# Order of loads on one DMA queue: the G load first in its group, weight rows a stage later, the first tile of the last pass in parts

## The chip, the cores and the metric

One core of a Trainium2 chip runs the whole program in one launch. The metric is device time in microseconds (us). PE is the matmul engine (PEld its weight loads), DVE the vector engine, ACT the scalar engine, POOL and SP the two others. SP does no arithmetic here: it issues DMAs, in the order of its instruction list. A DMA issued by SP or ACT goes through that engine's hardware queue, one issued by POOL through the software queue.

## The reference

The function returns the output of a forward pass and the gradients of all its inputs.

```python
def _fwd_reference(A_u, ..., B_w1, B_w3, B_w2):
    x = A_u                                   # [1, 2048, 576] bf16
    xn = _layernorm(x, axis=-1)
    s = _A_ref(xn, A_re, A_im, B_re, B_im, C_re, C_im, log_dt, Dskip)   # long convolution, 128 states
    g = _silu(_B_ref(xn, B_w1, B_w3, B_w2))   # FFN: (silu(xn w1) * (xn w3)) w2, F = 4608
    return x + s * g

def reference(...):
    _out, _vjp = jax.vjp(_f, ...)
    _grads = _vjp(grad_out)
    return (_out, *_grads)
```

The part that matters here is the backward pass of the FFN. With the stored G = xn w1 and U = xn w3 and the gradient `go` of the FFN's output it forms gh = go w2^T, from it the gradients GG and GU of G and U (with silu and its derivative), the weight gradients xn^T GG, xn^T GU and h^T go, and at last, token tile by token tile, GG w1^T + GU w3^T, which is added to the gradient from the convolution and sent through the layernorm's backward. Beside it run the sums for the gradients of the convolution's parameters.

## The kernel before, in words

2048 tokens are 16 tiles of 128; F = 4608 is 36 blocks of 128. The forward pass, in which G and U are written to DRAM (`G_dram`, `U_dram`), and the convolution's backward come first. The change lies in `backward` (L1519) and `phase6_inputs` (L1875), the last 650 us or so.

**The groups.** F is cut into NG = 18 groups of 256 columns (two blocks). In group `gi`, `phase6_group` (L1756) is a generator that yields named stages:

- h0 to h3: `make(s)` multiplies the output gradient `goT` with the group's transposed w2 (`w2T`, L1778, PE), ACT copies the result (L1781), DVE multiplies it into `gu` and `gg` (L1796);
- stored: two stores each of GU and GG to `GU_dram` and `GG_dram` (L1801);
- out_11_c and out_10_c, with marks out_11 and out_10: the weight gradients with the xn tiles (L1850, PE), each copied by ACT (L1852) and stored (`out_dram<-gw`);
- end: the last 64 rows of both (L1859, L1861), copied by ACT (L1864) and stored by `tail` (`out_dram<-gw13t`).

Between the stages the loop in `backward` puts in: the w2 gradient (`phase6_grad2`, L1819, copy by ACT L1823), the loads for later groups, the preparation of the next group (`phase6_prep`: ACT's Silu L1746 and its derivative L1749 on the next group's G, DVE's products L1742, L1743), and the steps of the parameter sums. The Silu of the next group is issued at h3, on ACT ahead of the copies of the stages that follow. PE writes these through two accumulators, which those copies empty.

**Buffers.** `gg_n`, `h_n` and `gu_n` each have two homes, taken in turn by the groups. In the last pass the same homes hold pieces of the transposed weights.

**Parameter sums.** 36 channels, each with two halves. `param_step` (L1230) issues a half: eight matmuls (L1398) with qT and gz, and DVE's product and sum (L1403, L1406) with pz. `param_loads` (L1377) loads qT (a DMA transpose), gz (two loads) and pz for a channel; after a channel's second half the channel two further on is loaded. From group 10 on (GP = 11) there are two to five halves in a group, and more in the last pass. At the end of the last group two such loads are held back, and `param_flush` issues them in the last pass.

**The order on SP.** From group GP - 1 = 10 on, `self.chain` makes every DMA that goes through `sp` follow the one before it in program order, and `one_queue` sends G, U and the gradient stores through SP too. A gradient store is put in a list and issued at the next stage (`stores_due`). The G load of the next group, which `phase6_load` (L1722) asks for at the start of a group, is also put off, to stage h0, where it comes behind the stores that are due:

```python
if stage == "h0" and self.gg_due:
    self.gg_due()
    self.gg_due = None
```

**wA and the pieces.** For the last pass w1 and w3 are needed transposed (block f as 128 x 576). Blocks 0 to 14 of w1 and 0 to 10 of w3 (`wA`) are loaded by rows of 128 (`load_wT_rows`), one chunk at stage end of each of groups 11 to 15. The other blocks come in pieces (`load_piece`) of 7 or 2 blocks, into homes as they come free in the last two groups and behind them. `load_acts` loads GG and GU of a token tile, transposed, as one DMA each of 36 blocks.

**The last pass.** `phase6_inputs` takes the tiles in the order 1, 3, 5, ..., 0, 2, ... For each, `product` runs 72 blocks x 2 column halves (L1899) into two accumulators. The first tile goes through the pieces in the order in which they stand in the list `wT`, up to `ready` = 49 blocks, then 14 more, then, after the first half of the second tile, the rest; later tiles take w1 then w3. `stops` are the blocks behind which a parameter half is put in. The output side (L1938 to L1971) and the blocks of the parameters' end (`phase5_step`, with `X_b`, `ST`, `WO_b`, whose DMAs go through POOL) run beside it.

## Time and profile before

| | us |
|---|---|
| runs | 1776.41, 1776.74, 1767.19 |
| median | 1776.41 |
| profiled execution | 1769.44 |
| its span | 1767.7 |
| PE busy, DVE busy, ACT busy, POOL busy | 1638.1, 1358.4, 937.4, 314.4 |
| granted clock of TensorE, mean | 0.988 |

The span is what the profile covers; the 1.7 us between it and the profiled execution's time lie around it. In rows of a timeline the first two numbers are start and length in us; a bracket at the end gives the idle time of that engine ahead of the row and what ended it. SPq rows are the issue of a DMA by SP, its waits included, not the transfer. In the profile L1899 is the product of the last pass, L1850 the weight gradients, L1693 every DMA transpose, L1717 the G load, L1828 the gradient stores, L1801 the stores of GG and GU.

### The profile page before, as it was taken

Reading aid. Unit: us, or ns where it says so; the run is one execution under the profiler, and the core shown is the slowest. Engines: PE = TensorE matmul, PEld = TensorE weight load, DVE = VectorE, ACT = ScalarE, POOL = GpSimd, SP = SyncE. Lnnn points to the kernel's source line nnn. Section 1 sums busy time; section 2 is a strip of 40 time slices with the busy share of each in tenths; the row PEclk is TensorE's granted clock in tenths of the full one; section 3 lists DMA queues with packets and bytes.
Section 4 is the critical chain, followed back from the end, with each engine's and each line's share of the span. In section 5 each row is a group of like instructions: output and inputs, shape, how many; then the busy total and the mean of one; then the engine's idle time right before and its main releaser. Section 6 shows DMA issues by size and latency. Waiting matters only on the chain. (4 is left out here: it accounts for less than half of the span.)

```text
span 1767.7 us, 35351 instructions
## 1 busy us (share of the span) xinstructions
PE 1638.1 (93%) x13849; PEld 1207.7 (68%) x13909; DVE 1358.4 (77%) x2102; ACT 937.4 (53%) x1757; POOL 314.4 (18%) x516
## 2 busy tenths in 40 slices
PE   7789988999999999999989899999898988999998
PEld 3445544544535777788878788878787876787886
DVE  8778888796783554988966989569797974888775
ACT  5789999976863112776746676555444511010101
POOL 3112222223134110111111101000000033031132
PEclk9999999999999999999999999999999999999999
DMA  7789998889699998867664756589897999999994
GB/s 221 269 268 366 349 355 302 307 267 298 224 274 244 228 204 188 218 206 214 193 189 153 221 167 207 168 225 244 204 239 198 225 244 236 224 219 240 219 213 93
DMA packets 644286, 411.98 MB, mean 233 GB/s; under 512 B 424422, under 2 KB 590934, under 8 KB 639510
## 3 DMA queue, kind: packets, MB, share of 16 engines
q1 hardware_dynamic: 593740, 303.40, 67.2%
q0 software_dynamic: 27632, 87.21, 15.3%
q10 hardware_dynamic: 22746, 19.10, 4.1%
q8 instruction: 109, 1.79, 0.4%
q14 instruction: 59, 0.48, 0.1%
HBM read 130.88 MB, written 190.89 MB: 182 GB/s over the span
## 5 line engine op out<-in xcount | busy, mean ns | idle before, releaser
L1899 PEld LDWEIGHTS <-acts 128*128 128x128 bf16 x2304 | 225.8, 99 | 69.5 <-issue 7.6
L1850 PEld LDWEIGHTS <-xn_bf 128*128 128x128 bf16 x2304 | 225.9, 98 | 56.9 <-issue 29.4
L1403 DVE TENSOR_TENSOR pr_q<-et_ps,pz 128x1024 f32<-128x1024 f32 x144 | 176.0, 1222 | 58.6 <-PE et_ps L1398 45.9
L1899 PE MATMUL px<-wT,acts 128*128 128x288 bf16 x1472 | 192.9, 289 | 7.4 <-DMA wT<-in_B_w_dram 7.4
L1032 PEld LDWEIGHTS <-xnT 128*128 128x128 bf16 x1152 | 107.0, 98 | 112.5 <-issue 24.5
L1406 DVE TENSOR_REDUCE S_all<-pr_q 128x32 f32<-128x1024 f32 x144 | 175.3, 1217 | 3.3
L1778 PE MATMUL ph<-w2T,goT 128*128 128x256 bf16 x1440 | 171.7, 273 | 3.1 <-ACT gh L1781 3.1
L1850 PE MATMUL pgw<-gu_n,xn_bf 128*128 128x256 bf16 x1152 | 137.0, 276 | 23.2 <-ACT gw L1823 19.7
L1032 PE MATMUL pg<-wmB_w,xnT 128*128 128x512 bf16 x545 | 149.1, 379 | 7.7 <-ACT g_t L1048 4.8
L1778 PEld LDWEIGHTS <-goT 128*128 128x128 bf16 x1440 | 139.7, 98 | 20.5 <-issue 4.3
L1819 PE MATMUL pgw<-go_o,h_n 128*128 128x288 bf16 x1152 | 152.3, 287 | 0.2 <-DVE h_n L1743 0.2
L1032 PE MATMUL pu<-wmB_w,xnT 128*128 128x512 bf16 x553 | 149.8, 379 | 0.8
L1819 PEld LDWEIGHTS <-h_n 128*128 128x128 bf16 x1152 | 112.6, 98 | 28.7 <-issue 0.8
L1850 PE MATMUL pgw<-gg_n,xn_bf 128*128 128x256 bf16 x1152 | 130.2, 273 | 1.2 <-ACT gw L1852 1.2
L1781 ACT CAST gh<-ph 128x512 bf16<-128x512 f32 x144 | 82.4, 603 | 77.9 <-PE ph L1778 66.2
L1955 ACT ACTIVATE go<-gx 128x576 bf16<-128x576 f32 x16 | 10.9, 683 | 209.0 <-DVE gx L1938 180.5
L1046 ACT ACTIVATE s_t<-pg 128x512 bf16<-128x512 f32 x144 | 87.9, 611 | 58.3 <-PE pu L1040 36.3
L1899 PE MATMUL px<-wA,acts 128*128 128x288 bf16 x832 | 109.1, 287 | 4.0 <-DMA acts<-GU_dram 2.7
L679 ACT ACTIVATE cs_k<-et_ps 128x512 bf16<-128x512 int16 x216 | 111.5, 637 | 0.1
L1742 DVE TENSOR_TENSOR gg_n<-gg_n,h_n 128x1024 bf16<-128x1024 bf16 x72 | 48.5, 684 | 57.0 <-ACT gg_n L1749 57.0
L1830 POOL DMA_DIRECT2D out_dram<-gw x40 | 26.2, 655 | 349.9 <-ACT gw L1852 166.3
L1060 POOL DMA_DIRECT2D U_dram<-u_t x72 | 51.8, 720 | 203.9 <-ACT u_t L1051 197.0
(315 smaller groups left out, 3231.2 us busy)
## 6 DMA issues: line engine op xcount, KB each, us to landing
U_dram<-u_t POOLq DMA_DIRECT2D x72, 256.0 KB, 4.9
H_dram<-h_t SPq DMA_DIRECT2D x72, 256.0 KB, 5.2
G_dram<-g_t POOLq DMA_DIRECT2D x72, 256.0 KB, 5.0
Q_dram<-q_k SPq DMA_DIRECT2D x36, 512.0 KB, 5.0
GG_dram<-gg_n SPq DMA_DIRECT2D x36, 512.0 KB, 9.9
GU_dram<-gu_n SPq DMA_DIRECT2D x36, 512.0 KB, 5.0
E_dram<-E_k SPq DMA_DIRECT2D x54, 256.0 KB, 2.5
E_l<-E_dram SPq DMA_DIRECT2D x36, 384.0 KB, 6.5
```

Of the source, the lines that this page charges most:

```text
L679: self.sin_last = nc.scalar.activation(out=CS[:, :, o:o + 256], in_=pt[:].bitcast(I16)[:, :, 0::2], func=ACT.Sin, scale=6.283184 / 2 ** 16)
L1032: ins = nc.tensor.matmul(pt[:], lhsT=xnT[:, c, ts], rhs=wm[w][:, c, :], start=(q == 0 and c == 0), stop=(q == 1 and c == nfull - 1))
L1046: nc.scalar.activation(out=s_t[:, :, q, :], in_=pgv, func=ACT.Silu)
L1060: self.u_stores[step] = nc.gpsimd.dma_start(out=dst[fb * ng:(fb + 1) * ng, :, i0:i0 + NT, :].rearrange("g p t f -> p g (t f)"), in_=src[:] ...
L1403: nc.vector.tensor_tensor(out=pr[:].rearrange("p r k e -> p r (k e)"), in0=T[x][:].rearrange("p z k h j a -> p (z k h j a)")[:, None].to_b ...
L1406: nc.vector.tensor_reduce(out=self.S_all[:].rearrange("p r (h c) -> p r h c", h=2)[:, :, :, d0:d0 + 2], in_=pr[:].rearrange("p r k (h j a) ...
L1742: nc.vector.tensor_tensor(out=gg[:, sl, :], in0=gg[:, sl, :], in1=hn[:, sl, :], op=ALU.mult)
L1778: self.pe_last = nc.tensor.matmul(ph[j][:, k, :].rearrange("p (a f) -> p a f", f=P), lhsT=lw, rhs=rh, start=(n == 0), stop=(n == nfull))
L1781: self.sc(lambda: nc.scalar.copy(out=gh[:, j], in_=ph[j][:]))
L1819: self.pe_last = nc.tensor.matmul(pgw[pi_][:, 0:pw], lhsT=hn[:, tt, fl * P:(fl + 1) * P], rhs=go_o[:, tt, po:po + pw], start=(tt == 0), st ...
L1850: self.pe_last = nc.tensor.matmul(pw_[:, 0:FG], lhsT=self.xn_bf[:, tt, c * P:(c + 1) * P], rhs=nat[:, tt, :], start=(tt == 0), stop=(tt == ...
L1899: self.pe_last = nc.tensor.matmul(px[pi_][:, 0:pw], lhsT=acts[i][:, ai, fi, :], rhs=w[:, po:po + pw], start=(n == 0), stop=(n == len(steps ...
```

## The change

1. The G load of the next group is issued at once when `phase6_load` asks for it, at the start of a group. On SP it then stands ahead of the stores that are due there.
2. The chunks of `wA` go from stage end of group g to stage h1 of group g + 1. On SP they stand behind the G load and the `gw13t` stores.
3. The first parameter channel is loaded at stage h2 of group 10, not behind the stores; the second stays.
4. `one_queue` ends with group 16: the gradient stores of the last group go through POOL.
5. GG and GU of the first tile of the last pass: blocks 0 to 33 of GG at h3 of the last group, those of GU behind the stores of the group, then the two last blocks of each.
6. The list of pieces is sorted up to its last four, w1 first, so that the first tile takes all early blocks of w1 before w3. GU of the second tile is loaded ahead of the last two pieces of w3 (blocks 11, 12 and 29 to 35).
7. `param_flush(1)` comes behind GU of the third tile, and the stops of the third tile are 20, 36, 52, 66.

The instructions of the engines stay as they are, but for two more DMA transposes, and on PE and DVE the first parameter half stands earlier.

```diff
-        FA = 12
...
-        FA, GP = 14, 11
+        GP, FE = 11, FT - self.FG // P
...
             for gi in range(NG):
-                self.chain = self.one_queue = gi >= GP - 1
                 lastg = gi == NG - 1
+                self.chain, self.one_queue = gi >= GP - 1, GP - 1 <= gi < NG - 1
...
                     self.stores_due()
-                    if stage == "h0" and self.gg_due:
-                        self.gg_due()
-                        self.gg_due = None
...
-                    if stage == "end" and 0 <= gi - GP < cfg.DT:
+                    if stage == "h1" and 0 <= gi - GP - 1 < cfg.DT:
                         for part in wT[0:2]:
-                            self.load_wT_rows(part, gi - GP)
+                            self.load_wT_rows(part, gi - GP - 1)
...
+                    if stage in ("h2", "stored") and gi == GP - 1:
+                        ch = int(stage == "stored")
+                        self.loaded[ch] = self.param_loads(ch)
                     if stage == "stored":
-                        if gi == GP - 1:
-                            for ch in range(2):
-                                self.loaded[ch] = self.param_loads(ch)
                         if lastg:
                             self.hold = []
                             self.phase5_turn()
-                            acts = [self.load_acts(0)]
+                            self.load_acts(0, (1,), acts[0], 0, FE)
+                            self.load_acts(0, (0, 1), acts[0], FE)
...
                         step()
+                        if lastg and stage == "h3":
+                            acts = [self.load_acts(0, (0,), None, 0, FE)]
...
             self.load_piece(wT, inp, "gg_n", 0, 29, 7)
+            self.load_acts(1, (1,), acts[1])
             self.load_piece(wT, wp, "w2T", 1, 11, 2)
             self.load_piece(wT, inp, "gu_n", 1, 29, 7)
-            self.load_acts(1, (1,), acts[1])
-            self.one_queue = False
-            self.stores_due()
+            wT[:-4] = sorted(wT[:-4], key=lambda part: part[0])
...
-    def load_acts(self, i, parts=(0, 1), t=None):
+    def load_acts(self, i, parts=(0, 1), t=None, f0=0, f1=None):
...
         for k in parts:
-            self.nat_transpose(t[:, k], (self.GG_dram, self.GU_dram)[k][self.order[i]])
+            self.nat_transpose(t[:, k, f0:f1], (self.GG_dram, self.GU_dram)[k][self.order[i]][:, f0 * P:(f1 or self.cfg.FT) * P])
...
         if self.one_queue:
-            self.gg_due = lambda: self.sp(lambda: self.nc.sync.dma_start(out=gg[:], in_=self.G_dram[gi]))
+            self.sp(lambda: self.nc.sync.dma_start(out=gg[:], in_=self.G_dram[gi]))
...
             acts.append(self.load_acts(2, (0,), acts[0]))
-            self.param_flush(1)
             product(1, opened[1][0], 0, cfg.FT, ())
             product(0, opened[0][0], n2, n3, ())
             self.load_acts(2, (1,), acts[0])
+            self.param_flush(1)
             acts.append(self.load_acts(3, (0,), acts[1]))
...
-                stops = ... (12, 28, 44, 62) if i == 2 else ...
+                stops = ... (20, 36, 52, 66) if i == 2 else ...
```

More of the change, by code (lines that the diff above doesn't have):

```diff
@@ L1555, in backward @@
             self.tail = None
-            self.one_queue, self.gg_due, self.due = False, None, []
+            self.one_queue, self.due = False, []
             self.at(T0 - TG)
@@ L1932, in phase6_inputs @@
                     self.ln_finish()
-                stops = () if i in (0, 1, LT - 1) else (12, 28, 44, 62) if i == 2 else (14, 38, 62) if 3 <= i <= 8 else (20, 50)
+                stops = () if i in (0, 1, LT - 1) else (20, 36, 52, 66) if i == 2 else (14, 38, 62) if 3 <= i <= 8 else (20, 50)
                 if i > 1:
```

## The prediction

> **What bounds the kernel now.** I read the page first, then the waits of PE from 1140 us on, since the diff touches nothing that is issued earlier.
>
> ```profile
> PE 1638.1 (93%) x13849; PEld 1207.7 (68%) x13909; DVE 1358.4 (77%) x2102; ACT 937.4 (53%) x1757; POOL 314.4 (18%) x516
> ...
> PE pgw L1850 <- ACT gw L1823: 15.8, 5, 7.2
> PE px L1899 <- DMA wT<-in_B_w_dram: 7.4, 1, 7.4
> PE et_ps L1398 <- DMA gz<-gK_dram: 6.6, 2, 3.3
> ...
> PE px L1899 <- DMA acts<-GU_dram: 2.7, 1, 2.7
> PE pgw L1850 <- DVE gg_n L1796: 1.6, 1, 1.6
> PE px L1899 <- DMA acts<-GG_dram: 1.3, 1, 1.3
> ```
>
> PE is the bound: busy 93% of the span. So only PE's idle time can be won, and nearly all of it here stands in three places: the weight-gradient matmuls of the late groups (15.8 and 1.6; us in total, times, longest), the start of the last pass (7.4, 2.7, 1.3), and two waits of the parameter halves (6.6 in two). The releaser "ACT gw L1823" is a middleman, so I went on to the timelines of PE, ACT and SP, one after the other.
>
> ```profile
> 1220.40 1.91 PE L1850 MATMUL pgw<-gu_n,xn_bf 128*128 128x256 bf16 x16 [1.61 <-DVE gg_n L1796]
> 1262.76 3.57 PE L1850 MATMUL pgw<-gu_n,xn_bf 128*128 128x256 bf16 x16 [7.25 <-ACT gw L1823]
> 1302.05 1.91 PE L1850 MATMUL pgw<-gu_n,xn_bf 128*128 128x256 bf16 x16 [2.40 <-ACT gw L1823]
> 1342.73 3.57 PE L1850 MATMUL pgw<-gu_n,xn_bf 128*128 128x256 bf16 x16 [5.57 <-ACT gw L1823]
> ...
> 1251.98 1.09 ACT L1781 CAST gh<-ph 128x512 bf16<-128x512 f32 x2 [1.10 <-PE ph L1778]
> 1260.07 1.28 ACT L1746 ACT_TABLE_LOAD   x1 [7.00 <-DMA gg_n<-G_dram]
> 1340.04 1.28 ACT L1746 ACT_TABLE_LOAD   x1 [5.32 <-DMA gg_n<-G_dram]
> ```
>
> ACT stands 7.00 us for the next group's G; the copy that empties PE's accumulator is queued behind that Silu, so PE stands 7.25. The two long stands also cost speed afterwards: the same 16 matmuls take 3.57 instead of 1.91.
>
> **Part A, the G load and the wA rows.** Why G is late is in SP's timeline, first of group 13, then of group 14:
>
> ```profile
> 1242.43 0.94 SPq L1828 DMA_DIRECT2D out_dram<-gw  x2
> 1243.42 4.44 SPq L1693 DMA_TRANSPOSE wA<-in_B_w_dram  x2
> ...
> 1252.86 1.14 SPq L1828 DMA_DIRECT2D out_dram<-gw13t  x2
> 1254.05 0.58 SPq L1717 DMA_DIRECT2D gg_n<-G_dram  x1
> ...
> 1289.09 4.54 SPq L1693 DMA_TRANSPOSE wA<-in_B_w_dram  x2
> ...
> 1294.99 0.53 SPq L1717 DMA_DIRECT2D gg_n<-G_dram  x1
> ```
>
> In the changed order the G load stands ahead of gw13t and the two wA transposes. In group 13 these are 4.44 + 1.14 us, with the gaps between rows about 5.7; in group 14 G moves from 1294.99 to 1289.09, 5.9. From issue to use took 1260.07 - 1254.05 = 6.0. So, with the same 6.0, G of group 13 lands at about 1254.4; ACT was free at 1253.07 (1251.98 + 1.09), which leaves 1.3 of the 7.00. In group 15 the 5.32 fall to nothing, and in group 14 PE's 2.40 are less than the 5.9. What PE can win at most: 1.61 + 7.25 + 2.40 + 5.57 = 16.8 of idle, and twice 3.57 - 1.91 = 3.3 of slow matmuls: 20.1. That is the upper end.
>
> What speaks for less is the DMA share of these stretches, cut at the ends of the groups (columns: busy us and count of PE, PEld, DVE, ACT, POOL; granted clock, DMA share, GB/s):
>
> ```profile
> 1202.00:1238.60 36.60, 34.95 (x346) 30.45 (x344) 32.99 (x37) 19.42 (x31) 0.00 (x0) 1.00 0.97 236
> 1238.60:1282.80 44.20, 36.91 (x348) 31.37 (x344) 33.22 (x37) 19.42 (x31) 0.00 (x0) 0.92 0.84 205
> 1282.80:1320.20 37.40, 34.95 (x348) 30.48 (x344) 33.01 (x37) 19.43 (x31) 0.00 (x0) 1.00 0.96 238
> 1320.20:1363.50 43.30, 37.73 (x350) 31.79 (x344) 33.08 (x37) 19.42 (x31) 0.00 (x0) 0.92 0.78 203
> ...
> 1438.00:1480.00 42.00, 30.71 (x239) 23.69 (x240) 17.22 (x43) 2.32 (x6) 21.68 (x42) 0.92 1.20 253
> ```
>
> Four groups take 161.5 us (36.6 + 44.2 + 37.4 + 43.3). Their transfers amount to 36.6 x 0.97 + 44.2 x 0.84 + 37.4 x 0.96 + 43.3 x 0.78 = 142.3 us at a share of 1. Without its stands PE would need 161.5 - 20.1 = 141.4, so the share would have to be 1.01. The highest share of these four rows is 0.97; at that, the four take 146.7, and the win is 14.8. The 1.20 further down shows that more than 1 exists with other transfers. A re-ordering brings no byte less, so I take the nearer rows: **15 us**, ends 8 (three quarters of G's advance eaten by queueing: 1.6 + 2.4 + half of 7.25, and nothing of 5.57) and 20.
>
> Behind the G load on SP stand gw13t, wA, then gw, w2T, the next h_n and the GU and GG stores. Everything from gw on keeps its place, since what moved ahead of wA was ahead of it already; in the groups without qT in between the qT load even gains. The wA rows are first read in the last pass, and the last of them go out at h1 of group 16, more than a group before: nothing. G's buffer was read last by the previous group's closing matmuls; SP reaches the new slot at 1243.4 against a group end of 1238.6, and at 1289.1 against 1282.8, so that wait is over before it begins.
>
> **Part B, the first parameter channel** is loaded at stage h2 of group 10 instead of after the stores, as the rows stood in SP's and PE's timelines:
>
> ```profile
> 1140.73 2.55 SPq L1693 DMA_TRANSPOSE w2T<-w2r  x2
> ...
> 1157.31 3.26 SPq L1693 DMA_TRANSPOSE qT<-Q_dram  x1
> ...
> 1163.63 0.69 PE L1398 MATMUL et_ps<-gz,qT 128*128 128x128 bf16 x8 [3.29 <-DMA gz<-gK_dram]
> ...
> 1502.93 1.01 PE L1398 MATMUL et_ps<-gz,qT 128*128 128x128 bf16 x8 [3.32 <-DMA gz<-gK_dram]
> 1504.70 6.08 PE L1899 MATMUL px<-wT,acts 128*128 128x288 bf16 x32
> 1525.67 4.08 PE L1899 MATMUL px<-wT,acts 128*128 128x288 bf16 x32
> ```
>
> By the order it now goes out ahead of the w2T row of 1140.73, 16.6 us before 1157.31, so the 3.29 goes; on PE these eight matmuls also move 41 matmuls ahead. Ends 0 and 3.3, taken **3**. On SP it now stands ahead of w2T, h_n and the stores of group 10, with 3.26 us of issue for qT and three small loads behind it (some 5 in all, an estimate: 3.26 and three issues of 0.58, the G row's); if that is not hidden, what follows is up to 5 us late. The same issues leave the queue after the stores, so only the order changes.
>
> **Part C, the start of the last pass.** SP's timeline, then the PE rows after it:
>
> ```profile
> 1431.16 4.85 SPq L1693 DMA_TRANSPOSE acts<-GG_dram  x1
> 1436.10 4.79 SPq L1693 DMA_TRANSPOSE acts<-GU_dram  x1
> ...
> 1447.14 4.30 SPq L1693 DMA_TRANSPOSE wT<-in_B_w_dram  x1
> 1451.48 2.39 SPq L1828 DMA_DIRECT2D out_dram<-gw  x4
> 1453.96 1.54 SPq L1828 DMA_DIRECT2D out_dram<-gw13t  x2
> 1455.60 10.77 SPq L1693 DMA_TRANSPOSE wT<-in_B_w_dram  x3
> ...
> 1464.25 3.52 PE L1899 MATMUL px<-wT,acts 128*128 128x288 bf16 x14 [7.42 <-DMA wT<-in_B_w_dram]
> ```
>
> 34 of 36 blocks of the first tile's GG go out at h3, before the last group's stores; GU follows behind the stores without waiting for them to land; only the last two blocks of each wait. GU is needed after 22 instead of 15 blocks, as the pieces of w1 now come first. Both waits, 1.3 + 2.7, should go. The 7.42 is for the piece gg_n (blocks 29 to 35 of w1), issued at 1455.60. The six stores ahead of it (2.39 + 1.54) go to the POOL queue, so it is issued 4 us earlier, and up to 4 more if GG's early issue (4.85) pulls the row forward; the two small transposes, at most 2.2 us each by the three-piece row (7, 2 and 7 blocks: 10.77 less twice 4.30), take that part back. Meanwhile PE comes 4 us earlier, so the stand mostly moves: PE wins what the transfer wins. The window 1438 to 1480 has a share of 1.20, the highest of all; there the transfer wins little. Ends 0 (the transfers are the limit) and 7.42 + 4.0 + 1.7 of slow clock (3.52, where 14 x 4.08 / 32 = 1.8 is usual) = 13; taken **4**.
>
> The Trainium skill, "DMA: Bandwidth & Descriptors", section "Issuing engines are not separate DMA queues", speaks against the move of the stores: transfers of all issuing engines share the same 16 DMA engines, so another queue saves only issue time. By that C is near its lower half; the share of 1.20 agrees. By the issue rows alone it would be 4 + 4.
>
> The POOL stores have their cover in POOL's idle time:
>
> ```profile
> 1434.79 4.17 POOL L1492 DMA_DIRECT2D out_dram<-WO_b  x8 [17.41 <-DVE WO_b L1487]
> ```
>
> Without that cover the X_b loads behind them come later by the issues of six stores, some 4 us by the SP rows (2.39 + 1.54), and DVE's parameter block with them, not PE's products.
>
> GU of the second tile is issued before the last two pieces of w3 now, and qT after GU of the third tile. Third-tile stops are moved from block 12, 28, 44, 62 to 20, 36, 52, 66, so the half that stood 3.32 at 1502.93 comes 8 blocks, 8 x 2 x 4.08 / 32 = 2.0 us, later on PE. **Part D**: the upper end is 3.32 + (6.08 - 4.08) = 5.3, the lower 0, should the channel come later by as much; taken **3**, the 2.0 and half of the slow clock.
>
> On that slow clock the Trainium skill, "TensorE: Matmul & The Clock Gate", section "HAM oscillation — how this bites in real kernels", says that an idle gap over some 3.4 us throttles the array again. The rows agree for 7.25, 5.57 and 7.42; they do not for 3.32, after which 6.08 stands for 4.08. By the rule the 1.3 left in group 13 costs no slow matmuls, and the sum holds.
>
> **Sum.** 15 + 3 + 4 + 3 = 25 us. The profiled execution took 1769.44 us (span 1767.7): 1744.4. The three runs before are 1776.41, 1776.74 and 1767.19, so their median is 7 above the profiled one and its fastest run 2 below; I put 1.6 on top, about a quarter of the 7: **1746**.
>
> **The rivals.**
> *PE is the only limit.* Transfers keep up as they do at 1.20, and nearly every stand goes: 20 + 3.3 + 10 + 5 = 38; 1769.4 - 38 + 1.6 = 1733. For it: the last pass runs at shares over 1 with a busy PE. Against it: no group row over 0.97. Chance 0.17.
> *The transfers hardly yield.* G is moved ahead in the queue, but it lands little earlier as the engines are full; A gives 8, B 3, C and D nothing: 11; 1760. For it: share 0.97 and 0.96 in the groups that hardly stand. Against it: 0.84 and 0.78 in those that do. Chance 0.20.
> *The order changes and the wait does not.* G is late for what lies before the moved entries (stores waiting for DVE); only B remains, 3: 1768. Against it: of the 10.6 us between 1243.42 and 1254.05, 4.44 and 1.14 belong to the entries that G passes. Chance 0.07.
> *Slower.* The G load heads its group, and everything on SP stands behind it until the previous group has released G's buffer on PE. Price: each us that SP is there before the group's end delays w2T, h_n and the stores of that group by as much. It decides from the point at which SP runs over 5 us earlier against PE than now (1243.4 - 1238.6 = 4.8): a stand of 6 us in each of five groups, against 20 won, gives 10 lost: 1781. Chance 0.06.
>
> **How the numbers follow.** The forecast, transfers at about 0.97 in the groups, has 0.50; its own range, with the ends of C and D about half used, is 1738 to 1754. The 8-in-10 range takes in most of the first two rivals: 1730 to 1763. A measurement of this kernel can tell about 0.5%, 9 us, from no change. Faster by more: 0.50 + 0.17 + 0.20 = 0.87. Within: 0.07. Slower: 0.06.
>
> **What would show it.** Right: the G row of SP directly behind the gw stores, ahead of gw13t; ACT's wait on G_dram in groups 13 and 15 under 2 us; no 3.57 row; group lengths of 35.5 to 37.5 us at a DMA share of 0.95 or more; no wait on GG_dram at the first product; a wait of 2 to 6 us on wT left there; et_ps without the 3.29. Wrong: group 13 still over 40 us with G issued early (transfers), PE waiting for w2T or h_n in the groups (order), ACT waiting on G with an idle DMA, or a wait on acts later in the last pass that was not there.

## The result, and the profile after

Twenty runs of the changed kernel have a median of 1769.72 us (1758.15 to 1792.69), twenty runs of the kernel before beside them 1778.91 (1767.19 to 1795.91). The ratio is 0.994, 95% interval 0.9911 to 0.9968: about 10.7 us faster, where 25 were forecast and 1746 us. The ratio leaves the slow runs of both kernels out; the medians, over all runs, are 9.2 us apart. The profiled execution took 1761.12 us.

```profile
span 1759.3 us, 35411 instructions
...
PE 1645.3 (94%) x13909; PEld 1208.4 (69%) x13909; DVE 1358.0 (77%) x2102; ACT 937.4 (53%) x1757; POOL 320.1 (18%) x524
```

The four late groups, cut at the weight load of each group's first product (columns as in the prediction):

```profile
1204.06:1239.59 35.53, 35.22 (x347) 30.45 (x345) 33.12 (x37) 19.44 (x32) 0.00 (x0) 1.00 0.97 240
1239.59:1276.32 36.73, 35.08 (x348) 30.46 (x346) 33.16 (x37) 19.41 (x32) 0.00 (x0) 1.00 0.95 240
1276.32:1311.85 35.53, 35.22 (x347) 30.46 (x345) 33.12 (x37) 19.44 (x32) 0.00 (x0) 1.00 1.01 234
1311.85:1353.16 41.31, 37.61 (x348) 31.74 (x346) 33.02 (x37) 19.40 (x32) 0.00 (x0) 0.92 0.97 235
sum 149.10, PE 143.13 PEld 123.11 DVE 132.42 ACT 77.69 POOL 0.00; mean PE 35.78 PEld 30.78 DVE 33.10 ACT 19.42 POOL 0.00
```

Cut in the same way, the kernel before takes 161.6 us; they have become 149.1. Three groups are as forecast; group 15 is not, and a stand has come in group 11. PE's rows at the gate products of groups 11, 13 and 15, and ACT's waits for G behind the last two:

```profile
1183.66 3.51 PE L1848 MATMUL pgw<-gu_n,xn_bf 128*128 128x256 bf16 x16 [2.78 <-ACT gw L1821]
1257.58 1.91 PE L1848 MATMUL pgw<-gu_n,xn_bf 128*128 128x256 bf16 x16 [1.61 <-ACT gw L1821]
1331.93 3.57 PE L1848 MATMUL pgw<-gu_n,xn_bf 128*128 128x256 bf16 x16 [3.70 <-ACT gw L1821]
...
1254.89 1.28 ACT L1744 ACT_TABLE_LOAD   x1 [1.36 <-DMA gg_n<-G_dram]
1329.25 1.28 ACT L1744 ACT_TABLE_LOAD   x1 [3.45 <-DMA gg_n<-G_dram]
```

Why G is late in group 15 is in SP's timeline. G does stand ahead of gw13t and wA, but two parameter channels stand ahead of G:

```profile
1309.60 1.68 SPq L1826 DMA_DIRECT2D out_dram<-gw  x1
1311.38 3.35 SPq L1691 DMA_TRANSPOSE qT<-Q_dram  x1
1314.78 1.87 SPq L1384 DMA_DIRECT2D gz<-gK_dram  x2
1316.69 0.59 SPq L1387 DMA_DIRECT2D pz<-PZ_dram  x1
1317.38 0.94 SPq L1826 DMA_DIRECT2D out_dram<-gw  x2
1318.41 2.85 SPq L1691 DMA_TRANSPOSE qT<-Q_dram  x1
1321.31 1.95 SPq L1384 DMA_DIRECT2D gz<-gK_dram  x2
1323.36 0.54 SPq L1387 DMA_DIRECT2D pz<-PZ_dram  x1
1323.94 0.42 SPq L1715 DMA_DIRECT2D gg_n<-G_dram  x1
...
1325.65 4.90 SPq L1691 DMA_TRANSPOSE wA<-in_B_w_dram  x2
```

The group begins at 1311.85, G goes out at 1323.94: 12.1 us behind, where it was 13.3 before (1334.08 against 1320.78). In group 13 the change takes it from 14.9 to 8.7. The same rows of the kernel before, group 15:

```profile
1320.30 1.22 SPq L1384 DMA_DIRECT2D gz<-gK_dram  x2
...
1323.24 5.21 SPq L1693 DMA_TRANSPOSE wA<-in_B_w_dram  x2
1328.54 2.33 SPq L1693 DMA_TRANSPOSE qT<-Q_dram  x1
1330.92 1.23 SPq L1384 DMA_DIRECT2D gz<-gK_dram  x2
...
1332.89 1.14 SPq L1828 DMA_DIRECT2D out_dram<-gw13t  x2
1334.08 0.58 SPq L1717 DMA_DIRECT2D gg_n<-G_dram  x1
```

The two channels stood ahead of G there too. G passes 5.21 + 1.14 us of entries and goes out 10.1 us earlier than in the first trace of the kernel before, but the group itself begins 8.9 us earlier, by what PE won in the groups ahead of it. SP has not come forward as much: the first channel's gz loads go out 2.9 us behind the group's start, where they went out 0.5 ahead of it, and the rows between them and G are longer (gz 1.87 and 1.95 for 1.22 and 1.23, qT 2.85 for 2.33).

The last pass, PE's stands:

```profile
1434.78 1.89 PE L1897 MATMUL px<-wA,acts 128*128 128x288 bf16 x14 [1.90 <-DMA acts<-GU_dram]
...
1447.44 6.50 PE L1897 MATMUL px<-wT,acts 128*128 128x288 bf16 x28 [4.98 <-DMA wT<-in_B_w_dram]
...
1491.24 1.01 PE L1398 MATMUL et_ps<-gz,qT 128*128 128x128 bf16 x8 [3.37 <-DVE S_all L1406]
...
1503.68 0.61 PE L1398 MATMUL et_ps<-gz,qT 128*128 128x128 bf16 x8 [1.55 <-DMA gz<-gK_dram]
...
1706.88 0.59 PE L1398 MATMUL et_ps<-gz,qT 128*128 128x128 bf16 x4 [3.82 <-DVE pr_q L1403]
1707.26 8.04 PE L1897 MATMUL px<-wT,acts 128*128 128x288 bf16 x42
```

The wait on GG at the first product is gone; the one on GU is 1.90 instead of 2.7, the one on wT 4.98 instead of 7.42. But the third tile's half that stood 3.32 stands 3.37 and again 1.55, and late in the pass, where the kernel before had no stand, 3.82 us and 8.04 us for 42 matmuls (5.31 is usual) are lost.

### The profile page after: what moved, and what is told of

The parts are those of the page before. It is cut to its first block, busy times and chain, and to the rows that moved or that the text cites. A ratio compares the mean times of both kernels' runs of the same rounds, so it can differ in the third digit from the quotient of the medians.

```text
span 1759.3 us, 35411 instructions
## 1 busy us (share of the span) xinstructions
PE 1645.3 (94%) x13909; PEld 1208.4 (69%) x13909; DVE 1358.0 (77%) x2102; ACT 937.4 (53%) x1757; POOL 320.1 (18%) x524
## 5 line engine op out<-in xcount | busy, mean ns | idle before, releaser
L1032 PE MATMUL pg<-wmB_w,xnT 128*128 128x512 bf16 x576 | 154.8, 380 | 5.7 <-ACT g_t L1048 4.7
L1032 PE MATMUL pu<-wmB_w,xnT 128*128 128x512 bf16 x576 | 154.7, 379 | 0.0
L1779 ACT CAST gh<-ph 128x512 bf16<-128x512 f32 x144 | 82.5, 603 | 77.6 <-PE ph L1776 67.6
```

The lines of the kernel that those rows point to most:

```text
L1032: ins = nc.tensor.matmul(pt[:], lhsT=xnT[:, c, ts], rhs=wm[w][:, c, :], start=(q == 0 and c == 0), stop=(q == 1 and c == nfull - 1))
L1779: self.sc(lambda: nc.scalar.copy(out=gh[:, j], in_=ph[j][:]))
```

## The experiments

Groups are counted from 0; in the expectations "the eleventh" and "the fifteenth" with a stand are groups 11 and 15, "the second and fourth late group" 13 and 15, and the stores behind which the first channel was loaded are group 10's. Times in us; the ratio is to the kernel before in the same comparison.

| run | median (lowest to highest) | ratio, interval |
|---|---|---|
| G first, wA later | 1776.31 (1756.96 to 1780.23) | 0.9985, 0.9953 to 1.0017 |
| last pass only | 1784.23 (1772.83 to 1799.44) | 1.0023, 0.9995 to 1.0051 |
| changed, last stores on SP | 1766.29 (1753.36 to 1781.73) | 0.9925, 0.9888 to 0.9961 |
| changed, again | 1768.80 (1760.22 to 1787.29) | 0.9963, 0.9936 to 0.9989 |
| before, channel loads out | 1748.21 (1743.02 to 1752.21) | 0.9808, 0.9772 to 0.9843 |
| changed, channel loads out | 1740.89 (1739.45 to 1745.07) | 0.9772, 0.9738 to 0.9806 |
| changed, first channel back | 1773.03 (1758.62 to 1789.17) | 0.9947, 0.9911 to 0.9982 |
| before, again | 1782.47 (1768.46 to 1787.93) | 0.9988, 0.9956 to 1.0020 |
| changed, late tiles on DVE | 1764.47 (1755.61 to 1776.92) | 0.9918, 0.9891 to 0.9945 |
| changed, last pass loads on ACT | 1765.41 (1760.51 to 1769.87) | 0.9925, 0.9894 to 0.9955 |
| changed, wA back | 1772.39 (1763.88 to 1795.27) | 0.9959, 0.9928 to 0.9990 |
| before, gz and pz cut to an eighth | 1763.34 (1757.24 to 1768.76) | 0.9891, 0.9854 to 0.9927 |
| before, gz and pz on ACT | 1759.18 (1755.23 to 1762.55) | 0.9870, 0.9833 to 0.9908 |
| changed, last pass loads on ACT, DVE | 1764.25 (1757.21 to 1766.44) | 0.9889, 0.9853 to 0.9925 |
| before, the same two | 1768.92 (1765.44 to 1777.29) | 0.9937, 0.9904 to 0.9970 |
| changed, gz and pz on ACT | 1756.65 (1752.19 to 1761.03) | 0.9871, 0.9834 to 0.9908 |
| the same, late tiles on DVE | 1757.68 (1752.04 to 1759.48) | 0.9872, 0.9838 to 0.9905 |
| G first, gz and pz on ACT, DVE | 1758.79 (1753.97 to 1764.67) | 0.9884, 0.9850 to 0.9919 |

### Parts of the change

G first and the wA rows a stage later, nothing else:

```diff
-            self.gg_due = lambda: self.sp(lambda: self.nc.sync.dma_start(out=gg[:], in_=self.G_dram[gi]))
+            self.sp(lambda: self.nc.sync.dma_start(out=gg[:], in_=self.G_dram[gi]))
-                    if stage == "end" and 0 <= gi - GP < cfg.DT:
+                    if stage == "h1" and 0 <= gi - GP - 1 < cfg.DT:
```

> The kernel before with two edits only: in groups 12 to 16 the G rows are issued at once instead of at stage h0, and the wA rows at h1 of the next group instead of at the end. Nothing else of the change. Theory 1 (the transfers of SP's queue are nearly always in flight, so that the order takes away only the stands): the long stands of TensorE before the gate product, 7.25 us in the second of the late groups and 5.57 us in the fourth, shrink by some 5 us and 2 us; TensorE reaches the gate product of the last group 12 to 15 us earlier than in the kernel before, and the whole kernel is 8 to 12 us shorter. Theory 2 (the order of the groups decides nothing, what the whole change wins comes from the start of the last pass): under 3 us. If a later stage takes it back, the gain at the last group is there and the kernel is 3 us shorter or less.

Groups 12 to 15 take 151.3 us against 161.6, with stands of 3.68 and 3.03 left: 10 us won, less than expected. At the end 2.7 are left (0.15% of 1777.8), with an interval that holds no change. In the trace the last pass gives it back (338.6 us from its first product to the end of the span, 328.5 and 327.0 before); but this trace is of the longest of its twelve runs, so how much of that is the change's stays open.

The rest of the change, with the group part as before:

> The changed kernel with its group part as in the kernel before: G at h0, wA rows at the end of the group, both channels of the parameters behind the stores of the eleventh group. Left of the change are the GG in two parts, its place, GU2, the order of the pieces and of the flush, and the last group's stores on POOL's queue. Theory 1: the last group ends as in the kernel before, the start of the last pass is 3 to 4 us shorter, the third tile wins nothing, and the kernel is 0 to 4 us shorter. If the late stand of the last pass (3.82 us before pr_q and 2.7 us of slow clock behind it in the changed kernel, where POOL stood 6.71 us for a load of X_b) belongs to this part, the kernel is 3 to 5 us longer than the one before; if it belongs to the chance of one execution, it isn't seen here.

The start of the last pass (to the 228th weight load behind its first product) is 38.3 us long; before it was 40.9 and, in the second trace, 41.4. The kernel as a whole does not gain. The late stand is seen at 1.77 us.

The last group's stores on SP again:

```diff
-                self.chain, self.one_queue = gi >= GP - 1, GP - 1 <= gi < NG - 1
+                self.chain = self.one_queue = gi >= GP - 1
...
+            self.one_queue = False
+            self.stores_due()
             wT[:-4] = sorted(wT[:-4], key=lambda part: part[0])
```

> The changed kernel, with the GG and GU stores of the last group and what follows on SP's queue as in the kernel before (chained up to the first matmuls of the last pass), instead of on their own queues. Theory 1: the start of the last pass has the same transfers in the same order, and the time stays within 2 us of the changed kernel. Rival: the stores on the other queue let GU's load begin early and are worth the whole of the 3.3 us won at the start of the last pass; then this kernel is 3 us longer than the changed one.

1766.29, and the intervals overlap: no loss can be seen, and none of 3 us is shut out. That the move of the stores gains anything is not shown.

The changed kernel and the one before, each a second time:

> The changed kernel a second time, for its spread and a second trace. If the stand of 2.78 us in the eleventh group and the 6.8 us lost late in the last pass belong to the change, both show again at the same lines; if they were chance, other places have them, and the milestones of TensorE up to the last group are 13 to 16 us ahead of the kernel before.

> The kernel before a second time, for a second trace of it. If the stand of 3 to 4 us before pr_q late in the last pass (near 1707 us in the changed kernel) is brought by the change, it is missing here again, as in the first trace; if it is the kernel's own and comes by chance of the execution, it is seen here, and so is a wait for GU or gz late in the last pass. The stands of the second and fourth late group are 5 to 8 us each, as in the first trace.

The stand in group 11 (2.39) and the late one (3.11) are there again, as are group 13's and 15's rests (3.36 and 2.79); the four groups take 150.8. In the six other runs that keep this order and these loads on SP they take 147.4 to 151.3. In the second trace of the kernel before they take 161.1, and the late stand is missing again. Here one caution: both traces of the kernel before come from runs far below its medians (1769.44 and 1768.46, medians 1778.91 and 1782.47), so what its usual last pass looks like, they do not show. In the second trace of the changed kernel three of PE's stands and two of SP's transposes in the last pass are:

```profile
1503.53 0.66 PE L1398 MATMUL et_ps<-gz,qT 128*128 128x128 bf16 x8 [2.12 <-DMA gz<-gK_dram]
1531.87 0.61 PE L1398 MATMUL et_ps<-gz,qT 128*128 128x128 bf16 x8 [1.21 <-DMA gz<-gK_dram]
...
1668.34 2.87 PE L1897 MATMUL px<-wA,acts 128*128 128x288 bf16 x22 [1.57 <-DMA acts<-GU_dram]
...
1513.91 9.51 SPq L1691 DMA_TRANSPOSE acts<-GG_dram  x1
...
1529.66 8.17 SPq L1691 DMA_TRANSPOSE acts<-GU_dram  x1
```

SP's rows stand there without a gap, and the same transpose that elsewhere holds SP for 4.7 us holds it 8 to 9.5; PE then waits for gz or GU. What holds SP longer, the rows don't tell.

The first channel's load back behind the stores:

```diff
-                    if stage in ("h2", "stored") and gi == GP - 1:
-                        ch = int(stage == "stored")
-                        self.loaded[ch] = self.param_loads(ch)
                     if stage == "stored":
+                        if gi == GP - 1:
+                            for ch in range(2):
+                                self.loaded[ch] = self.param_loads(ch)
```

> The changed kernel with the first parameter channel loaded behind the stores of the eleventh group again, as before. Theory 2 (loading it at h2 only moves the wait: 3.3 us won at the first channel, 2.8 us of standing and up to 1.6 us of slow clock paid 20 us later, in the eleventh group's gate product): the time stays within 2 us of the changed kernel, the stand of 3.3 us on gz is back and that of 2.4 to 3.1 us before the gate product of the eleventh group is gone. If the early load is worth the 3 us of the forecast, this kernel is 3 us longer than the changed one.

The stand on gz is back with 3.44 us, that of group 11 down to 0.45. From group 10's first product to group 12's the kernel before takes 76.7 and 76.8 us, the changed one 75.6 and 75.2, this one 76.8: the early load is worth 1.1 to 1.6 us, not 3. The whole times don't separate that from nothing.

The wA rows back at the end of their group:

```diff
-                    if stage == "h1" and 0 <= gi - GP - 1 < cfg.DT:
+                    if stage == "end" and 0 <= gi - GP < cfg.DT:
                         for part in wT[0:2]:
-                            self.load_wT_rows(part, gi - GP - 1)
+                            self.load_wT_rows(part, gi - GP)
```

> The changed kernel with the wA rows at the end of their group again; G is issued first thing. It splits part A. By the issue rows G stands behind 4.44 us of wA in groups 13 to 16 again, so if the place in the queue decided, groups 12 to 15 are some 4 us longer in each group with a stand, 8 us in all, and the kernel too. By theory 1 (the transfers' sum decides) the four groups take 147 to 152 us as in the changed kernel, and the time stays within 3 us.

156.0 us for the four groups, between the two expectations: about half of what the groups win is the wA rows' place. The whole times (1772.39 against 1769.72, intervals overlapping) don't show it.

### Transfers or SP's issue

The channels' loads left out:

```diff
     def param_loads(self, ch):
+        if ch >= 2:
+            return self.loaded[ch % 2]
```

> The kernel before with the loads of the parameter channels (qT, gz, pz) left out from the third channel on; their arithmetic runs on the first two channels' data. That takes some 7 transfers' worth per group from SP's queue in groups 11 to 16 and in the last pass; everything else is unchanged. Theory 1 (the transfers set the pace of groups 12 to 16 and of the last pass, where they run at a share of 0.95 and more): the stands before the gate products in the second and fourth late group shrink by 3 us or more each, those on gz, GU and wT in the last pass go or shrink, and the kernel is 12 to 25 us shorter than the one before. Rival (the order in SP's queue sets the stands): the stands of 7.25 and 5.57 us stay within 1.5 us, and the kernel is under 8 us shorter.

> The changed kernel with the same loads left out as in the one before it. Theory 1: the rest of the stands in groups 12 to 16 (1.61 and 3.70 us) goes below 0.5 us, PE keeps in the last pass what it won in the groups, as no wait on gz, GU or wT over 1 us is left behind the start; the kernel is 5 to 20 us shorter than the changed one. Against the lightened kernel before the gain is then at least the forecast's part A without the transfers, 15 us or more, if the transfers were what ate it; if it is 10 us or less with idle transfers, something other than the transfers took the gain back.

In the old order, with the loads out, there is no stand at all in groups 12 to 15:

```profile
sum 142.17, PE 140.94 PEld 121.83 DVE 132.53 ACT 77.63 POOL 0.00; mean PE 35.24 PEld 30.46 DVE 33.13 ACT 19.41 POOL 0.00
```

The changed kernel takes the same 142.2. So the order of G and wA gains nothing here once the channels' loads are gone. At the end it is 7.3 us ahead of the old one by the medians (7.0 in the two traces), though it is 12.3 ahead at the 228th weight load behind the first of the last pass (1443.54 against 1455.79); in the tile behind it PE stands 10.53 us for DVE's pr_q, where it stands 7.03 in the old one. With these loads out DVE is what PE waits for next. These two runs took bytes and issues away at once; two more part these. First the bytes alone (pz goes into the tile of the channel two back):

```diff
+            n = 512 if ch < 2 else 64
+            # gz: ...[:, 0:n] on both sides; pz: the same with an eighth of its columns
```

> The kernel before with gz and pz of every channel from the third on cut to an eighth of their bytes; the same DMAs are issued at the same places on SP, qT is whole. Per group of 2.5 channels it takes 0.84 MB of 8.8 from the transfers. Theory 1 (bytes): at the 237 GB/s of the changed kernel's groups that is 3.5 us a group; groups 12 to 15 take 147 to 152 us instead of 161.6, the stands of 7.25 and 5.57 fall below 4. Theory 4 (SP's issue time): the four groups take 159 us or more.

```profile
sum 158.03, PE 146.28 PEld 125.02 DVE 132.49 ACT 77.69 POOL 0.00; mean PE 36.57 PEld 31.25 DVE 33.12 ACT 19.42 POOL 0.00
```

3.5 us of 161.6, with stands of 6.25, 2.17 and 2.97. As a whole this kernel is 17.6 us faster at the median. The groups don't hold that much, so bytes may count in the last pass; but the traces don't show it there (325.9 us from its first product on, against 328.5 and 327.0 before). Then the issues alone, all bytes moved:

```diff
+            ld = (lambda f: f(nc.scalar)) if ch >= 2 else (lambda f: self.sp(lambda: f(nc.sync)))
-            self.sp(lambda: nc.sync.dma_start(out=gK[...], in_=self.gK_dram[...]))
+            ld(lambda e: e.dma_start(out=gK[...], in_=self.gK_dram[...]))
...
-        self.sp(lambda: nc.sync.dma_start(out=pz[:]..., in_=self.PZ_dram[:, ch]...))
+        ld(lambda e: e.dma_start(out=pz[:]..., in_=self.PZ_dram[:, ch]...))
```

> The kernel before with gz and pz of every channel from the third on issued on ACT's queue; all bytes are moved. It takes some 2 us a channel, 4.7 us a group, out of SP's row. Theory 4 (SP's issue time): groups 12 to 15 take 147 to 154 us instead of 161.6, and the waits on gz and GU in the last pass go. Theory 1 (bytes): the four groups take 158 us or more. If ACT's work behind the loads comes late, ACT's rows show it, and the groups are longer than 162.

149.05 us, and the kernel is 1.3% faster than before, where the change wins 0.6%. SP's rows ahead of G in group 13 (which begins at 1244.29), and PE's gate product behind them:

```profile
1242.95 4.75 SPq L1694 DMA_TRANSPOSE wA<-in_B_w_dram  x2
1247.80 2.32 SPq L1694 DMA_TRANSPOSE qT<-Q_dram  x1
1250.21 1.18 SPq L1829 DMA_DIRECT2D out_dram<-gw13t  x2
1251.48 0.54 SPq L1718 DMA_DIRECT2D gg_n<-G_dram  x1
...
1260.94 2.07 PE L1851 MATMUL pgw<-gu_n,xn_bf 128*128 128x256 bf16 x16 [0.27 <-ACT gw L1824]
```

G stands behind wA and qT as ever, and yet the 7.25 are gone: SP is there earlier. The stands of 2.2 us that this kernel has in groups 12 and 14 are ACT's own: pz waits in its queue for DVE's product with the last channel, and the copies of gh behind it. That waiting edge cost 3.17 us of ACT in group 12:

```profile
1219.81 0.33 ACTq L1388 DMA_DIRECT2D pz<-PZ_dram  x1
1220.23 1.07 ACT L1782 CAST gh<-ph 128x512 bf16<-128x512 f32 x2 [3.17 <-DVE pr_q L1404]
```

The same on the changed kernel:

> The changed kernel with gz and pz of every channel from the third on issued on ACT's queue. Theory 4 (SP's issues ahead of G): the 3.7 us ahead of G in the eleventh and fifteenth group go from SP's row, G is issued 8 us or less behind the group's first product, the stands of 2.8 and 3.7 us there fall below 1, and groups 12 to 15 take 142 to 146 us. Theory 1 (by now the transfers): they take 148 us or more. The kernel is 5 to 10 us shorter than the changed one by the first, and by what the last pass wins through SP alone, some 4 us, by the second.

```profile
sum 145.76, PE 140.72 PEld 121.83 DVE 132.56 ACT 77.36 POOL 0.00; mean PE 35.18 PEld 30.46 DVE 33.14 ACT 19.34 POOL 0.00
```

145.8: transfers did not hold the changed kernel at 149. What is left over 142.2 are ACT's two stands of 2.12 and 2.21. G goes out 2.6 to 3.2 us behind the start of each group. In group 11 the expectation missed: the stand of 2.8 at the gate product is gone, but earlier in the group PE stands 4.23 us for ACT's copies of gh, which come behind gz loads that hold ACT 4.12 us.

The move puts the loads on a second queue besides taking their issues from SP, and no run has the one without the other. But with seven eighths of their bytes gone from SP's queue the groups of the kernel before win 3.5 us, with the issues gone 12.5, so the bytes in that queue are the smaller part. Nor is a long SP row all issuing: in group 12 of the changed kernel the two GG stores hold SP 6.90 us and the two GU stores of the same size 1.03, with the data of both ready (DVE's last gg_n ends at 1222.06):

```profile
1227.23 1.03 SPq L1799 DMA_DIRECT2D GU_dram<-gu_n  x2
1228.35 6.90 SPq L1799 DMA_DIRECT2D GG_dram<-gg_n  x2
```

What SP waits for in such a row stays open.

The lag of G's issue behind the group's first product, and PE's stand at the gate product, side by side:

| lag / stand, us | group 12 | 13 | 14 | 15 |
|---|---|---|---|---|
| before | 11.0 / 1.61 | 14.9 / 7.25 | 11.7 / 2.40 | 13.3 / 5.57 |
| changed, wA back | 9.1 / 1.31 | 13.2 / 5.11 | 10.8 / 2.43 | 11.6 / 3.46 |
| G first, wA later | 6.1 / 0.27 | 9.3 / 3.68 | 5.9 / 0.27 | 10.7 / 3.03 |
| changed, again | 6.0 / 0.27 | 11.3 / 3.36 | 5.4 / 0.27 | 11.0 / 2.79 |
| changed | 5.7 / 0.27 | 8.7 / 1.61 | 6.8 / 0.27 | 12.1 / 3.70 |
| before, loads on ACT | 7.8 / 2.20 (ACT) | 7.2 / 0.27 | 8.4 / 2.20 (ACT) | 8.0 / 0.27 |
| changed, loads on ACT | 2.6 / 2.12 (ACT) | 2.7 / 0.27 | 2.6 / 2.21 (ACT) | 3.2 / 0.27 |
| before, loads out | 3.8 / 0.27 | 3.8 / 0.27 | 4.7 / 0.27 | 3.7 / 0.27 |

Up to a lag of about 8 us PE does not stand for G (0.27 is there in every group of the table without a longer stand); at 8.7 to 12.1 us it stands 1.3 to 3.7, at 13 to 15 us 5 to 7. That holds whatever brings the lag about: order, issues or loads left out. The lag is not all of it: at like lags of 9 to 12 us groups 12 and 14 stand less than 13 and 15, and in two runs outside the table group 12 has lags of 10.0 and 10.3 and no stand.

### The last pass

Loads of the last pass on ACT (as above with `ch >= 18`):

> The changed kernel, with the gz and pz loads of channels 18 to 35, those of the last pass, issued on ACT's queue instead of SP's; qT stays. It takes three issues of 0.53 to 0.62 us and their gaps, about 2 us a channel and some 4 us a tile of 19.3 us, out of SP's row, which stands without a gap there. Theory 4 (SP's issue time paces the last pass): the waits for gz, GU and wT behind the third tile go, and the kernel is 4 us or more shorter. Theory 1 (the transfers pace it, whichever queue they come from): SP's transposes take longer by as much as is taken out, and the time stays within 3 us of the changed kernel. If ACT's own work comes late behind the loads, it is longer.

1765.41, 4 us under the changed kernel at the median, with overlapping intervals. Behind the third tile no wait on gz or GU is left, and SP's row has gaps; DVE stands PE up instead:

```profile
1507.26 5.12 SPq L1692 DMA_TRANSPOSE acts<-GU_dram  x1
1515.37 4.53 SPq L1692 DMA_TRANSPOSE acts<-GG_dram  x1
...
1494.14 0.38 PE L1399 MATMUL et_ps<-gz,qT 128*128 128x128 bf16 x4 [3.87 <-DVE pr_q L1404]
...
1550.52 0.69 PE L1481 MATMUL et_ps<-ident_f,ST 128*128 128x128 f32 x4 [2.37 <-DVE ST L1467]
```

The late stand: in the first trace of the changed kernel POOL stood 6.71 us at a load of X_b, behind it the output side's operations of that tile, and DVE waited for those (POOL, then DVE):

```profile
1698.09 0.99 POOL L1461 DMA_DIRECT2D X_b<-in_A_C_re_dram  x2 [6.71 <-issue]
...
1704.87 0.82 DVE L1969 SCALAR_TENSOR_TENSOR go<-gx,rstd,gxs 128x576 bf16<-128x576 f32 x1 [10.50 <-POOL gxs L1964]
```

```diff
-        eng = nc.gpsimd if i + 1 < cfg.LT else nc.vector
+        eng = nc.gpsimd if i < 12 else nc.vector
```

> The changed kernel, with the three small output-side operations (sc twice, gxs plus go) of tiles 12 to 15 on DVE instead of POOL, where they stand behind loads of X_b that wait 6 us. Theory 3 (the gain is given back late in the last pass through POOL: the X_b loads stand behind X_b stores that land late, DVE waits 10 us for gxs, the parameter half behind it, and TensorE 3 to 4 us for that, with a slow clock after it): the stand before pr_q near 1707 us goes, and the kernel is 4 to 6 us shorter than the changed one. If the parameter half is late for another reason, the stand stays and the time is within 2 us or, by some 1.3 us of DVE work in each of four tiles, longer.

1764.47, 5 us under the changed kernel at the median, as expected, but with overlapping intervals. In the trace the late stand is gone: POOL still stands 5.75 us, and DVE no longer waits for it:

```profile
1701.16 0.82 DVE L1969 SCALAR_TENSOR_TENSOR go<-gx,rstd,gxs 128x576 bf16<-128x576 f32 x1
...
1701.81 0.98 POOL L1461 DMA_DIRECT2D X_b<-in_A_C_re_dram  x2 [5.75 <-issue]
```

From PE's 1835th weight load behind the first of the pass (1700.12 in the trace before) to the end of the span takes 67.4 us here; 67.6 and 68.2 before; 74.2 and 72.3 in the changed kernel; 74.5 with G first alone, whose last pass is the old one. So the loss comes without the new start of the pass too; with that start alone it is 69.3. With the loads on ACT, cut or left out it is 67.4 to 67.7 in every trace.

Both together, on either kernel:

> The changed kernel with both edits that helped the last pass: gz and pz of channels 18 to 35 on ACT's queue, and the small output-side operations of tiles 12 to 15 on DVE. If the two losses are separate (waits for gz, GU behind the third tile; the late stand before pr_q), the gains add: 8 to 10 us under the changed kernel, 1758 to 1762 at the median, 18 us under the one before. If DVE, which already stood TensorE up for 3.9 and 2.4 us with the loads on ACT, is next, it is 5 us or less.

> The kernel before with the same two edits as in the run ahead of this one, and nothing of the change. It tells what the change is worth where the last pass gives little back: if the last pass ate the change's gain, the changed kernel with these edits is 12 to 15 us faster than this one; if the gain of the groups was never more than what is seen at the end, 8 to 10.

They don't add: 1764.25, and DVE's stands of 4.56 and 2.25 are the next. Against the kernel before with the same edits the change wins 4.7 us at the medians, neither of the two expected figures, and the intervals overlap. With all loads of gz and pz on ACT, the remaining two versions:

> As the run ahead of this one, and the small output-side operations of tiles 12 to 15 on DVE. If the late stand before pr_q comes with the loads on ACT too, it goes here and wins another 4 to 5 us; the run with loads on ACT in the last pass alone did not show it, and then this one is within 2 us of the one ahead.

> The kernel before with G first and the wA rows a stage later, gz and pz from the third channel on on ACT's queue, and the output-side operations of tiles 12 to 15 on DVE; the last pass and its start as before. It leaves out what the loads on ACT made worse in the changed kernel: waits of 2 us in the last group and of 3.9 and 2.4 us for DVE in the last pass. If the start of the last pass is worth 3 to 4 us there, it is 3 to 4 us longer than the run ahead of it; if the change's new start costs DVE's stand, it is 2 to 5 us shorter, at 1750 to 1757.

1757.68 and 1758.79; with 1756.65 (the changed kernel, gz and pz on ACT) and 1759.18 (the old one) they can't be told apart. All four are below both kernels, by 11 to 13 us below the changed one at the medians; the intervals of all but 1758.79 stand just clear of the changed kernel's 0.9911 to 0.9968. With SP relieved, the change is worth 2.5 us at the medians, within what the intervals leave open.

## Why the prediction was wrong, by its own steps

**The start.** The forecast subtracted from 1769.44 + 1.6; the kernel before has a median of 1778.91. Of the 23.7 us between 1746 and 1769.72, 7.9 are that step: the profiled execution was among the fastest, and a quarter of its distance was too little. Of the 25 us, parts A to D come to 14 to 17 as measured below, while the medians are 9.2 apart; by that estimate some 5 to 7 were lost in the last pass, whose later tiles the sum put at nothing.

**Part A, taken 15, measured 10.3 to 12.5** (161.6 and 161.1 against 150.8 and 149.1; G first alone 10.2). "Of the 10.6 us ... 4.44 and 1.14 belong to the entries that G passes" was right, and so was the 1.3 left of ACT's 7.00 in group 13 (1.36 in the first trace). The step that failed is "in group 15 the 5.32 fall to nothing": 3.45 were left, since two channel loads, 3.35 + 1.87 + 0.59 and 2.85 + 1.95 + 0.54 us of SP, still stand ahead of G. The step took G's advance against the old time of the group. The 5.21 + 1.14 us of entries that G passes would have left a lag of about 7 of the 13.3; it was 12.1, because PE comes to group 15 8.9 us earlier and SP comes to those loads later against PE than before. Without gz and pz on SP the lag is 3.2 there and the stand is gone. The prediction shows SP's rows of groups 13 and 14, not of 15.

**What was held to be the limit.** The sum took a DMA share of 0.97 as the end. The share did come to 0.95 to 1.01, but it was no limit: with all bytes moved and the issues on ACT the four groups of the changed kernel take 145.8 and those of the kernel before 149.0, and with fewer bytes and the same issues those of the kernel before still take 158.0. The rival "the transfers hardly yield", 1760, is nearer in its total, but its reason is wrong too. Nearest in its total is "the order changes and the wait does not", 1768; that is luck, as it lets the groups win nothing and starts from the same low base. Its reason, entries ahead of the moved ones, was in part right for groups 13 and 15, but named stores, where it is the channels' loads. The slower one did not come: the G row holds SP 0.42 to 1.53 us, so at most about 1.1 us of waiting for its buffer can be in it.

**Part B, taken 3, measured 1.1 to 1.6.** The 3.29 went, and the price that was named but set at nothing was paid in group 11: 2.78 us of standing and 3.51 instead of 1.91 for 16 matmuls.

**Part C, taken 4, measured 2.5** in the means of two traces each (41.1 before, 38.6 after). "The stand mostly moves" was right: 7.42 became 4.98 (in the second traces 6.87 and 5.97).

**Part D, taken 3, measured 0 at best.** The halves that stood 3.32 before stand 3.37 for DVE and 1.55 for gz; in the second trace it is 3.22 and 2.12.

**The last pass** is the other step that failed: the sum took it as unchanged behind the third tile, without a reason. It lost: from its first product to the end of the span 332.0 and 337.9 us in the changed kernel, 328.5 and 327.0 before. Since those two traces are of runs 9 and 14 us below their medians, how much of this belongs to the change stays open. What it consists of is shown: waits on gz and GU behind a gapless SP row, and POOL's chain at the end.

**The two rules cited.** The Trainium skill, "DMA: Bandwidth & Descriptors", section "Issuing engines are not separate DMA queues", was used to set another queue's worth low: it saves only issue time, which is usually small beside the DMA. That it saves issue time agrees; that this is small does not hold here, for with gz and pz on ACT the kernel before went from 1780.91 to 1759.18. By the other rule, of the Trainium skill's "TensorE: Matmul & The Clock Gate", section "HAM oscillation — how this bites in real kernels", gaps under some 3.4 us should leave the clock alone. Here 2.78 us was followed by 3.51 for 16 matmuls (granted clock 0.62 from 1183 to 1187.5), and 3.70 by 3.57 (0.50 from 1331 to 1335.5); the stand of 1.61 in group 13 was followed by 1.91, as the prediction had it.

## What to carry to other kernels

Where one in-order queue issues everything, the question for a late load is not only what its move passes, but how far behind its consumer the queue is when it gets there; tabulate that lag for every round, not for the one with the longest stand. A DMA share near 1 is no proof that bytes are the limit: cut the bytes with the issues kept, then move the issues with the bytes kept. And look at the spread before trusting one profiled execution as the base of a sum.

## What the runs showed of the hardware

One transpose of the last pass, the same 36 blocks, held SP between 4.66 and 11.12 us in rows of the changed kernel's two traces, waits included. With gz and pz on ACT's queue the spread of the kernel's times fell as well: 1755 to 1763 and 1752 to 1761 in six runs each, against 1771 to 1804 and 1766 to 1794 in the thirteen and eleven runs of the kernel before beside them. The slow clock after a stand has no sharp edge here: 2.78 us brought 3.51 for 16 matmuls, 3.68 us in the kernel with G first 2.61, 2.17 us in the one with cut loads 3.56, and 2.40 us in the kernel before the usual 1.91.
